# First batch's attention of a fused attention and mixture-of-experts kernel: where the exponentials are divided by their sums

## The chip, the cores and the metric

The kernel runs on one core of a Trainium2 chip. Its time is device microseconds of one launch, and the median of the runs of a kernel is what is compared. The engines are TensorE (PE in the profile, with its weight loads as PEld), VectorE (DVE), ScalarE (ACT), GpSimd (POOL) and SyncE (SP), which issues the DMAs.

## The reference, cut to what matters

Two batches, 8 heads, 768 positions, head dimension 64. Queries and keys that belong to the same of 16 clusters see each other; the result of the attention goes through two dense stages. Only the attention is touched by the change:

```python
    scores = scale * np.matmul(q, k.transpose(0, 1, 3, 2))
    scores = np.where(mask, scores, -1000000000.0)
    scores = scores - np.max(scores, axis=-1, keepdims=True)
    attn = np.exp(scores)
    attn = attn / (np.sum(attn, axis=-1, keepdims=True) + 1e-09)
    return np.matmul(attn, v).astype(np.float32)
...
    attn_out = _attn_ref(**attn_kwargs)
    x = np.ascontiguousarray(attn_out.transpose(0, 2, 1, 3)).reshape(B * S, H * D)
    x = _moe_ref(x=x, **moe_kwargs)
    return _moe2_ref(x=x, **moe2_kwargs)
```

## The kernel before, in words

The program is a list of tasks, each with an engine, a length, a priority and the buffers that it reads and writes. A planner in the kernel (`Order.plan`) places them one after the other by priorities and lengths from the table `PAR`, and the engines then run their instructions in that order, each engine strictly in its own. So a change of tasks or of numbers in the table moves instructions of all engines.

Batch 0 runs its attention alone at the start (up to about 150 us), beside the conversion of the dense weights (wconv), which fills gaps on ScalarE, GpSimd and VectorE. Then come the dense stages of batch 0, between whose products the attention of batch 1 is put, and the dense stages of batch 1.

The attention of batch 0 is the method `turned`. It works on pairs of heads (hp, four of them) and blocks of 256 queries (blk, three of them): 12 blocks, in the order of the list `seq`. A block has four units: two heads (q) by two groups of 128 queries (j). For a unit:

- TensorE makes the scores (pss, L827 and L829, 128 x 768 in two PSUM banks; two such buffers).
- VectorE takes the negated maximum of each row (L834), ScalarE the exponential with the sum of each row (e, L835; the trace shows the read of the sum as an instruction of its own).
- VectorE adds 1e-9 to the sum and takes the reciprocal (method `sums`, L843 and L844), and GpSimd multiplies the 128 x 768 exponentials with it in place (L735).
- TensorE turns them in six transposes (pst, L747, in two halves of three), and ScalarE (L754) or VectorE (L756) copies each half to SBUF (pt), by the letters of `kt`: A is ScalarE, D is VectorE.

When the four units of a block are there, TensorE multiplies values and turned exponentials (psv, L763): 12 products of 64 rows and 256 columns, the two heads into the two halves of the rows. They are issued in six parts. ScalarE takes the scaled high half of the result (x1h, L771) and VectorE the low half (x1l, L772), both from PSUM. The dense layer reads x1h and x1l (psg, L976 to L978).

New pairs of heads are prepared between the units: products with the centroids (psc, psct, pso), the splits of queries and keys (qa, ka, kb), and DMAs for them.

Of the kernel before, what the change touches and what calls it, by code (L numbers as in the profile page):

```python
# [9 lines left out]
F32 = mybir.dt.float32  # L10
# [11 lines left out]
PSC = 1024.0  # L22
# [5 lines left out]
def _f32(u):  # L28
# [14 lines left out]
    wx=-1.1522284557866715,  # L43
    wxs=1.4523186816394191,
    wx0=43.37150067903462,
    wl=7.46084025153843,
    slack=0.05,
    vre=2,
    nbv=12.297071615165793,
    nbr=16.02553508875921,  # L50
# [6 lines left out]
    ta=33.594464710837215,  # L57
    tu=2.610847985583524,
    lead0=24.37119650954177,
    lead2=1.612592269486031,  # L60
    vlead2=-5.510083383690325,
    lead1=2.0943943567986207,
    vlead=-47.653832407507394,
    avp=-10.148156292544726,
    parts=3,
    avpa=-4.563255851914643,
    kn='PPPPPP',
    kt='AAADA',
    kb='AAPD',
    gl=["DDDD", "DDDD"],  # L70
    mx=28.217289639625243,
    sp=15.01076876764054,
    spc=8.604011088911196,
    wse=dict(i="P", o="S", **{"1": "P", "2": "A"}),
    v0=9.16094046643471,
# [3 lines left out]
    v1=-23.758591458339424,  # L79
    a_pool=dict(raw=2, vr=4, sc=1, so=1, cs=2, oh=3, sm=2, e=7, pt=5, tiny=11, stk=4),  # L80
    b_pool=dict(raw=2, vr=2, sc=1, so=1, cs=1, oh=1, sm=2, e=2, p=3, pt=3, vh=1, vl=1, tiny=11, stk=2),
    xbb=1,
    loa="VP",
    lob="VV",
    r64p=2.853890633309904,
    slow=1.1738599594625483,
# [3 lines left out]
    trp=5.099669873070424,  # L90
    trh=2,
    parta=6,
    cv0=131.63876951108648,
    cvd=17.514404477757832,
# [10 lines left out]
    seq=[0, 1, 3, 2, 5, 4, 6, 7, 9, 10, 11, 8],  # L105
    btail=7.85293067823645,
    bu0=40.446540415353034,
    bdu=31.34254887856145,
    bvl=4.7901688951714965,
    bpr=6.264441884379736,  # L110
# [270 lines left out]
def body(ctx: ExitStack, tc: tile.TileContext, qk, vd, cent, w_in, w_out, probs, w1, w2, out):  # L381
# [33 lines left out]
    def pool(n, prio, fn, r, w, ns=2.1):  # L415
        return add("POOL", 1e-3 * (n * ns + 150), prio, fn, r, w, lk=True)
# [150 lines left out]
    class Attn:  # L567
# [824 lines left out]
```

## Time and profile before

| what | us |
|---|---|
| median of 3 runs | 969.84 |
| lowest and highest run | 967.96, 970.83 |
| profiled execution, its own time | 969.13 |
| its span, first to last instruction | 967.4 |
| TensorE busy (weight loads) | 923.6 (545.8) |
| VectorE, ScalarE, GpSimd busy | 737.5, 646.5, 361.6 |

The profiled execution is 1.7 us longer than its span and 0.7 us below the median. A busy TensorE is not one at its peak: a product counts from its start to its modelled end, so consecutive ones overlap in the trace, and what a product costs is read from start to start.

### The profile page before, as it was taken

The page shows a single profiled execution, that of the slowest core. Times are in us where ns is not written, and L with a number is a line of the kernel's source. Part 1 is how long each engine was busy: PE and PEld are TensorE (multiplying, and loading weights), DVE is VectorE, ACT ScalarE, POOL GpSimd, SP SyncE. Part 2 cuts the span into 40 slices and gives each one's busy share as a digit, 9 for nine tenths or more (in the row PEclk, how much of TensorE's full clock was granted, in tenths as well). Part 3 has the DMA queues.
Part 4 walks back from the last instruction along what each step waited for, and adds up shares of the span by engine and source line. Part 5 has one row for each costly group of instructions (what it writes and reads, how often), then busy time and mean ns, then how long its engine had stood idle before and what let it go on. Part 6 is the DMA issues. An engine that isn't in the chain of part 4 may idle for free.

```text
span 967.4 us, 16161 instructions
## 1 busy us (share of the span) xinstructions
PE 923.6 (95%) x5627; PEld 545.8 (56%) x5627; DVE 737.5 (76%) x1551; ACT 646.5 (67%) x1311; POOL 361.6 (37%) x394
## 2 busy tenths in 40 slices
PE   3999999999989998999999999999999999999998
PEld 1767765655545654555565565566654555555554
DVE  8988795887779898798898988945589666554543
ACT  5899986867776787787897755565466554555421
POOL 2566744324434346445354321101234442334100
PEclk9999999999999999999999999999999999999999
DMA  8343439785535465467466579332111212212001
GB/s 246 107 135 91 140 101 319 263 279 183 175 119 173 83 133 134 129 127 173 122 116 159 156 163 226 106 110 86 36 66 66 88 63 69 87 45 87 1 1 66
DMA packets 124369, 121.63 MB, mean 126 GB/s; under 512 B 81472, under 2 KB 81472, under 8 KB 124288
## 3 DMA queue, kind: packets, MB, share of 16 engines
q1 hardware_dynamic: 124288, 120.61, 43.8%
q8 instruction: 44, 0.72, 0.3%
q14 instruction: 37, 0.30, 0.1%
HBM read 81.32 MB, written 14.68 MB: 99 GB/s over the span
## 4 chain that ended last, share of the span: by engine, by line
PE 46%; DVE 6%; ACT 3%; DMA 1%; issue 1%; POOL 1%; SPq 0%; POOLq 0%; ACTq 0%
PE psm L976 6%; PE psm L977 6%; PE psm L978 6%; PE psw L1053 6%; PE psw L1055 6%; PE psw L1054 6%; PE psg L977 2%; PE psg L978 2%; PE psg L976 2%; PE pss L827 1%; DMA wraw<-in_w 1%; PE psv L809 1%; PE pss L829 1%; DVE h L1217 1%; ACT e L835 1%
## 5 line engine op out<-in xcount | busy, mean ns | idle before, releaser
L882 POOL TENSOR_TENSOR w<-wraw,w 128x512 f16<-128x512 f32 (+1 forms) x128 | 136.1, 1083 | 188.9 <-ACT w L881 146.9
L976 PE MATMUL psm<-w,h 128*128 128x512 f16 x384 | 146.1, 381 | 2.7 <-DVE h L1217 2.5
L978 PE MATMUL psm<-w,h 128*128 128x512 f16 x384 | 146.1, 380 | 0.5 <-DVE h L1217 0.5
L977 PE MATMUL psm<-w,h 128*128 128x512 f16 x384 | 145.9, 380 | 0.0
L835 ACT ACTIVATE e<-pss,ut 128x768 f32<-128x768 f32 x96 | 86.3, 900 | 26.8 <-DVE ut L834 24.7
L834 DVE TENSOR_REDUCE ut<-pss 128x1 f32<-128x768 f32 x96 | 91.3, 952 | 11.2 <-PE pss L829 9.8
L1063 ACT ACTIVATE keep<-psw 128x384 f32<-128x384 f32 x96 | 46.6, 486 | 60.1 <-PE psw L1055 59.5
L881 ACT ACTIVATE w<-wraw 128x512 f16<-128x512 f32 (+1 forms) x128 | 71.7, 580 | 21.2 <-POOL wraw L880 12.4
L880 POOL TENSOR_SCALAR wraw<-wraw,wsc 128x512 f32<-128x512 f32 x64 | 48.3, 762 | 98.3 <-DVE ws L938 30.8
L976 PE MATMUL psg<-g,w 128*128 128x384 f16 x256 | 83.5, 326 | 1.4 <-DVE t L1124 1.2
L977 PE MATMUL psg<-g,w 128*128 128x384 f16 x256 | 83.4, 326 | 1.4 <-DVE g L1126 1.4
L978 PE MATMUL psg<-g,w 128*128 128x384 f16 x256 | 83.5, 326 | 0.0
L1239 DVE SCALAR_TENSOR_TENSOR oa<-psm,pq,oa 128x512 f32<-128x512 f32 x84 | 61.9, 744 | 23.6 <-PE psm L978 23.5
L977 PEld LDWEIGHTS <-w 128*128 128x128 f16 x512 | 50.1, 98 | 36.6 <-issue 5.4
L978 PEld LDWEIGHTS <-w 128*128 128x128 f16 x512 | 50.1, 98 | 36.0 <-issue 3.0
L976 PEld LDWEIGHTS <-w 128*128 128x128 f16 x512 | 50.7, 99 | 33.4 <-issue 1.7
L827 PE MATMUL pss<-ka,qa 128*128 128x384 f32 x192 | 61.5, 402 | 3.7 <-ACT e L835 3.1
L1217 DVE SCALAR_TENSOR_TENSOR h<-psw,h 128x384 f16<-128x384 f32 x78 | 42.9, 552 | 27.8 <-ACT h L1216 27.6
L978 PEld LDWEIGHTS <-h 128*128 128x128 f16 x384 | 37.6, 98 | 46.3 <-DVE h L1217 1.0
L1054 PE MATMUL psw<-tx,ws 128*128 128x384 f16 x192 | 63.0, 328 | 0.8 <-DVE tx L1005 0.8
L1053 PE MATMUL psw<-tx,ws 128*128 128x384 f16 x192 | 63.1, 328 | 0.7 <-ACT tx L1004 0.6
L1055 PE MATMUL psw<-tx,ws 128*128 128x384 f16 x192 | 63.0, 328 | 0.0
(198 smaller groups left out, 2370.1 us busy)
## 6 DMA issues: line engine op xcount, KB each, us to landing
wraw<-in_w SPq DMA_DIRECT2D x128, 256.0 KB, 3.5
r<-in_w_in SPq DMA_DIRECT2D x16, 512.0 KB, 4.5
r<-in_w_out SPq DMA_DIRECT2D x16, 512.0 KB, 4.6
w<-hl_i SPq DMA_DIRECT2D x32, 256.0 KB, 3.0
w<-hl_o SPq DMA_DIRECT2D x32, 256.0 KB, 4.0
raw<-in_qk SPq DMA_DIRECT2D x16, 384.0 KB, 3.9
vr<-in_vd SPq DMA_DIRECT2D x12, 384.0 KB, 4.1
hl_i<-w SPq DMA_DIRECT2D x16, 256.0 KB, 2.4
```

Source lines behind the costliest of these rows:

```text
L827: nc.tensor.matmul(ps[:, f, 0:HS], qa[:, qs], ka[:, f * HS:f * HS + HS], start=True, stop=False)
L834: dve(S, p, lambda: nc.vector.tensor_reduce(out=nb(), in_=ps[:, :, 0:HS], axis=AX.XY, op=ALU.max, negate=True), [ps], [(tb, n)])
L835: act(S, p, lambda: nc.scalar.activation(out=e.t.rearrange("p (a b) -> p a b", a=2), in_=ps[:, :, 0:HS], func=AF.Exp, bias=nb(), scale=1.0 ...
L881: act(c, p, lambda w=w, raw=raw, c=c: nc.scalar.activation(out=w[:, 0, 0:c], in_=raw[:, 0:c], func=AF.Copy), [raw], [(w, 0)])
L882: pool(c, p, lambda w=w, raw=raw, c=c: nc.gpsimd.tensor_tensor(out=w[:, 1, 0:c], in0=raw[:, 0:c], in1=w[:, 0, 0:c], op=ALU.subtract), [raw ...
L976: nc.tensor.matmul(o_, ah, bh, start=i == 0, stop=False)
L977: nc.tensor.matmul(o_, ah, bl, start=False, stop=False)
L978: nc.tensor.matmul(o_, al, bh, start=False, stop=i == 3)
L1053: nc.tensor.matmul(o_, ah, bh, start=not more and k == 0, stop=False, skip_group_check=more)
L1054: nc.tensor.matmul(o_, ah, bl, start=False, stop=False, skip_group_check=more)
L1055: nc.tensor.matmul(o_, al, bh, start=False, stop=k == 1, skip_group_check=more)
L1239: dve(512, p, lambda: nc.vector.scalar_tensor_tensor(out=oa[:, t], in0=ps.t, scalar=q, in1=oa[:, t], op0=ALU.mult, op1=ALU.add), [ps, qk], ...
```

## The change

In `turned` the exponentials of a unit are no longer multiplied with the reciprocals of their sums; the transposes read them as the exponential left them. The sums of the four units of a block lie in one tile (ut), and `sums` runs once on its four columns. Four new products (L763 in the new numbering, function `over`) multiply each column of reciprocals, repeated 64 times, with the 128 x 128 identity: the result has the reciprocal of query k in column k of each of 64 rows. They go to columns 256 to 511 of the PSUM tile psv, whose columns 0 to 255 take the product with values. ScalarE copies them to SBUF (r, with the scale that the result had), VectorE multiplies the product with values by r (u), ScalarE takes the high half from u, and GpSimd subtracts it for the low half. The letters of `kt` give VectorE 3 copies in 10 instead of 1 in 5, the order of blocks `seq` differs in two places, and most real numbers of the planner's table differ.

```diff
-    kn='PPPPPP',
-    kt='AAADA',
+    xl0='P',
+    kt='AADAAAADAD',
...
-    seq=[0, 1, 3, 2, 5, 4, 6, 7, 9, 10, 11, 8],
+    seq=[0, 1, 3, 5, 2, 4, 6, 7, 9, 10, 8, 11],
...
+            tb = self.buf("tiny", [128, 8], F32, "ut")
...
-                    tb = self.buf("tiny", [128, 8], F32, "ut")
-                    e = self.scores(qa, qb, ka, kb, blk * BQ + j * 128, tb, 0, p(i))
-                    self.sums(tb, 1, p(i), 1.0)
-                    sc = lambda eng, e=e, tb=tb: eng.tensor_scalar(out=e.t, in0=e.t, scalar1=tb[:, 2:3], scalar2=1.0, op0=ALU.mult, op1=ALU.mult)
-                    if PAR["kn"][i % len(PAR["kn"])] == "P":
-                        pool(S, p(i), lambda sc=sc: sc(nc.gpsimd), [(tb, 2)], [e], ns=0.956)
-                    else:
-                        dve(S, p(i), lambda sc=sc: sc(nc.vector), [(tb, 2)], [e], fast=True)
+                    e = self.scores(qa, qb, ka, kb, blk * BQ + j * 128, tb, i, p(i), 4)
...
-            ps = Buf(p_v[b], [128, BQ], F32, "psv")
+            ps = Buf(p_v[b], [128, 2 * BQ], F32, "psv")
...
+            def over():
+                for j in range(JQ):
+                    for q in range(2):
+                        c = BQ + 128 * j
+                        nc.tensor.matmul(ps[64 * q:64 * q + 64, c:c + 128], tb[:, 4 + q * JQ + j:5 + q * JQ + j].to_broadcast([128, 64]), ident.t,
+                                         start=True, stop=True, skip_group_check=True)
...
+            self.sums(tb, 2 * JQ, p(4), 1.0, 4)
+            pe(JQ * 0.235, p(4) + avp, over, [(tb, 4 + i) for i in range(2 * JQ)], [(ps, 1)], JQ * 512)
...
-            act(BQ, p(6), lambda: nc.scalar.activation(out=xh[:, hp, sl], in_=ps.t, func=AF.Copy, scale=sc), [ps, ks], [(xh, key)], ps=True, ap=True)
-            dve(BQ, p(6), lambda: nc.vector.scalar_tensor_tensor(
-                out=xl[:, hp, sl], in0=ps.t, scalar=sc, in1=xh[:, hp, sl], op0=ALU.mult, op1=ALU.subtract), [ps, ks, (xh, key)], [(xl, key)], ap=True)
+            u, r = self.buf("u", [128, BQ], F32), self.buf("u", [128, BQ], F32, "r")
+            act(BQ, p(5), lambda: nc.scalar.activation(out=r.t, in_=ps[:, BQ:2 * BQ], func=AF.Copy, scale=sc), [(ps, 1), ks], [r], ps=True, ap=True)
+            dve(BQ, p(6), lambda: nc.vector.tensor_tensor(out=u.t, in0=ps[:, 0:BQ], in1=r.t, op=ALU.mult), [(ps, 0), r], [u])
+            act(BQ, p(6), lambda: nc.scalar.activation(out=xh[:, hp, sl], in_=u.t, func=AF.Copy), [u], [(xh, key)])
+            low = lambda eng: eng.tensor_tensor(out=xl[:, hp, sl], in0=u.t, in1=xh[:, hp, sl], op=ALU.subtract)
+            if PAR["xl0"] == "P":
+                pool(BQ, p(6), lambda: low(nc.gpsimd), [u, (xh, key)], [(xl, key)])
```

In the planned order, TensorE's rows around the third block's product with values, before (pst the transposes, pss the scores, psv the product with values; an x behind a row counts instructions):

```order
L747 MATMUL pst<-ident,e 128x128 x6
L827 MATMUL pss<-ka,qa 128x384 x2
L829 MATMUL pss<-kb,qb 128x384 x2
L747 MATMUL pst<-ident,e 128x128 x3
L763 MATMUL psv<-pt,vr 64x256 x12
L747 MATMUL pst<-ident,e 128x128 x6
```

The same place after, in the new line numbers, where psv<-ident,ut are the four products that spread the reciprocals:

```order
L741 MATMUL pst<-ident,e 128x128 x3
L836 MATMUL pss<-ka,qa 128x384 x2
L838 MATMUL pss<-kb,qb 128x384 x2
L741 MATMUL pst<-ident,e 128x128 x6
L763 MATMUL psv<-ident,ut 64x128 x4
L836 MATMUL pss<-ka,qa 128x384 x2
L838 MATMUL pss<-kb,qb 128x384 x2
L757 MATMUL psv<-pt,vr 64x256 x12
L741 MATMUL pst<-ident,e 128x128 x6
```

The four products came in behind the last transposes of the block, apart from the product with values; of the 12 sets one, the last, stands directly ahead of its product with values.

VectorE's rows at the same time, before (L834 the maximum, L843 the addition, L844 the reciprocal, L959 to L963 the conversion of weights, L772 the low half):

```order
L843 TENSOR_SCALAR ut<-ut 128x1
L844 RECIPROCAL ut<-ut 128x1
L772 SCALAR_TENSOR_TENSOR x1l_585<-psv,vm,x1h_571 128x256
L834 TENSOR_REDUCE ut<-pss 128x1
L756 COPY pt<-pst 128x384
L834 TENSOR_REDUCE ut<-pss 128x1
L843 TENSOR_SCALAR ut<-ut 128x1
```

and after, for the third block (L843 is now the maximum, L852 the addition and L853 the reciprocal on four columns, L968 and L970 the conversion, L750 the copy):

```order
L843 TENSOR_REDUCE ut<-pss 128x1
L968 TENSOR_SCALAR wconv<-wconv 128x512
L970 SCALAR_TENSOR_TENSOR wconv<-r_615,wconv 128x512
L852 TENSOR_SCALAR ut<-ut 128x4
L843 TENSOR_REDUCE ut<-pss 128x1
L853 RECIPROCAL ut<-ut 128x4
L843 TENSOR_REDUCE ut<-pss 128x1
L750 COPY pt<-pst 128x384
```

Addition and reciprocal stand once per block now, and here a maximum stands between the two.

## Rows read from the trace of the kernel before

**Rows 1.** Stretches: us, busy of PE, PEld, DVE, ACT, POOL; PEclk, DMA, GB/s
```profile
29.60:149.20 119.60, 113.22 (x824) 84.55 (x823) 103.23 (x245) 110.21 (x246) 69.62 (x76) 1.00 0.39 117
150.00:200.00 50.00, 50.00 (x313) 30.46 (x312) 33.83 (x71) 36.75 (x72) 22.43 (x28) 1.00 0.86 301
200.00:300.00 100.00, 94.54 (x567) 55.19 (x566) 81.51 (x164) 74.97 (x156) 39.95 (x48) 0.98 0.55 183
```

**Rows 2.** Timeline of PE from 82 us: start, us, instruction; scores and transposes
```profile
82.92 0.60 PE L827 MATMUL pss<-ka,qa 128*128 128x384 f32 x2
...
83.70 0.82 PE L747 MATMUL pst<-ident,e 128*128 128x128 f32 x6
84.35 0.44 PE L827 MATMUL pss<-ka,qa 128*128 128x384 f32 x1
```

**Rows 3.** Timeline of PE from 95.6 us: the product with values and its neighbours
```profile
96.51 0.49 PE L747 MATMUL pst<-ident,e 128*128 128x128 f32 x3
96.93 2.81 PE L763 MATMUL psv<-pt,vr 128*64 128x256 f32 x24
99.68 0.88 PE L747 MATMUL pst<-ident,e 128*128 128x128 f32 x6
```

**Rows 4.** Timeline of PE, three short stretches inside that product
```profile
97.20 0.60 PE L763 MATMUL psv<-pt,vr 128*64 128x256 f32 x4
...
97.42 0.60 PE L763 MATMUL psv<-pt,vr 128*64 128x256 f32 x4
...
99.36 0.39 PE L763 MATMUL psv<-pt,vr 128*64 128x256 f32 x2
```

**Rows 5.** Groups by line, PE, 29.6 to 147.1 us: busy, mean ns, idle before
```profile
L747 PE MATMUL pst<-ident,e 128*128 128x128 f32 x279 | 40.9, 278 | 3.0 <-POOL e L735 1.9 <-POOL wconv L957 0.6 <-ACT pt L754 0.5
L763 PE MATMUL psv<-pt,vr 128*64 128x256 f32 x288 | 34.0, 383 | 0.0
L827 PE MATMUL pss<-ka,qa 128*128 128x384 f32 x88 | 26.6, 384 | 2.0 <-ACT e L835 1.5
...
L977 PE MATMUL psg<-x1l,w 128*128 128x384 f16 x11 | 3.6, 326 | 0.0
...
L632 PE MATMUL psc<-raw,ct 128*32 128x384 f32 x16 | 1.7, 498 | 0.0
L683 PE MATMUL pso<-ident_b,oh 128*64 128x128 bf16 x18 | 1.5, 222 | 0.0
```

**Rows 6.** Waits, 29.6 to 149.5 us: who for whom, total us, times, longest
```profile
PEld pss L827 <- ACT e L835: 5.5, 15, 1.0
...
PEld pst L747 <- POOL e L735: 3.6, 7, 1.5
...
PE pst L747 <- POOL e L735: 1.9, 3, 1.1
...
PEld pst L747 <- POOL wconv L957: 0.8, 1, 0.8
```

**Rows 7.** Groups by line, 25 to 150 us, of POOL and ACT
```profile
L735 POOL TENSOR_SCALAR e<-e,ut 128x768 f32<-128x768 f32 x48 | 45.9, 960 | 36.3 <-DVE ut L843 11.1 <-DVE wconv L959 3.7 <-PE pss L829 3.4
...
L754 ACT ACTIVATE pt<-pst 128x384 f32<-128x384 f32 x76 | 34.8, 493 | 3.3 <-PE pst L747 3.1
...
L771 ACT ACTIVATE x1h<-psv,vm 128x256 f16<-128x256 f32 x12 | 5.7, 473 | 1.1 <-PE psv L763 1.0
```

**Rows 8.** Timeline of all engines from 96.6 us: a maximum, and exponential to reciprocal
```profile
96.71 0.96 DVE L834 TENSOR_REDUCE ut<-pss 128x1 f32<-128x768 f32 x1 [0.19 <-PE pss L829]
...
97.76 0.90 ACT L835 ACTIVATE e<-pss,ut 128x768 f32<-128x768 f32 x1 [0.48 <-DVE ut L834]
...
98.79 0.15 DVE L843 TENSOR_SCALAR ut<-ut 128x1 f32<-128x1 f32 x1 [0.39 <-ACT e L835]
98.97 0.17 DVE L844 RECIPROCAL ut<-ut 128x1 f32<-128x1 f32 x1
```

**Rows 9.** Line L961, 25 to 150 us: durations in ns, min, median, max
```profile
L961 DVE SCALAR_TENSOR_TENSOR wconv<-r,wconv x16: 668/683/1086, 31.8 to 149.1; 128x512 int32<-128x512 int32 x16
```

More of the change, by code (lines that the diff above doesn't have):

```diff
@@ L56 @@
     wgap=4,
[L57 to L64, printed above, removed]
+    ta=37.644627171937636,
+    tu=2.618105922827514,
+    lead0=23.811664523217768,
+    lead2=1.3177589412550317,
+    vlead2=-6.734196292615577,
+    lead1=1.6382475212753322,
+    vlead=-81.01415307879348,
+    avp=-14.807207563391803,
     parts=3,
-    avpa=-4.563255851914643,
-    kn='PPPPPP',
-    kt='AAADA',
+    avpa=-5.248976072211778,
+    xl0='P',
+    kt='AADAAAADAD',
     kb='AAPD',
     gl=["DDDD", "DDDD"],
-    mx=28.217289639625243,
-    sp=15.01076876764054,
-    spc=8.604011088911196,
+    mx=28.184025027324456,
+    sp=14.78416087479403,
+    spc=2.4836840744754025,
     wse=dict(i="P", o="S", **{"1": "P", "2": "A"}),
-    v0=9.16094046643471,
+    v0=17.35296956647561,
     lr=0.3,
@@ L89 @@
     dpx=2,
[L90 removed]
+    trp=4.004466787339696,
     trh=2,
     parta=6,
[L93 to L94 removed]
+    cv0=132.11254764398825,
+    cvd=17.98889306697888,
     cva=2,
@@ L762, in av @@
                     for q in range(2):
-                        nc.tensor.matmul(ps[64 * q:64 * q + 64], vr[:, q, t], pts[q][:, :, t], start=t == 0, stop=t == NT - 1)
+                        nc.tensor.matmul(ps[64 * q:64 * q + 64, 0:BQ], vr[:, q, t], pts[q][:, :, t], start=t == 0, stop=t == NT - 1, skip_group_check=True)
+            def over():
[4 more added lines that the diff above has]
+                                         start=True, stop=True, skip_group_check=True)
             for part in range(parts):
-                pe(NT / parts * (BQ * 4 / 2400 + 0.02), p(4 + part * 4 / parts) + avp, lambda part=part: av(part), pts + [vr], [ps], NT / parts * BQ * 4)
+                pe(NT / parts * (BQ * 4 / 2400 + 0.02), p(4 + part * 4 / parts) + avp, lambda part=part: av(part), pts + [vr], [(ps, 0)], NT / parts * BQ * 4)
+            self.sums(tb, 2 * JQ, p(4), 1.0, 4)
+            pe(JQ * 0.235, p(4) + avp, over, [(tb, 4 + i) for i in range(2 * JQ)], [(ps, 1)], JQ * 512)
             sl = slice(blk * BQ, blk * BQ + BQ)
@@ L819, in block, with scores @@
                 out=xl[:, hp, sl], in0=ps.t, scalar=col, in1=xh[:, hp, sl], op0=ALU.mult, op1=ALU.subtract), [ps, (xh, key)], [(xl, key)])
-        def scores(self, qa, qb, ka, kb, q0, tb, n, p):
+        def scores(self, qa, qb, ka, kb, q0, tb, n, p, s0=2):
             ps = Buf(p_s[self.b], [128, 2, 512], F32, "pss")
@@ L836, in scores, with sums @@
                 out=e.t.rearrange("p (a b) -> p a b", a=2), in_=ps[:, :, 0:HS], func=AF.Exp, bias=nb(), scale=1.0, accum_out=rs()),
-                [ps, (tb, n)], [e, (tb, 2 + n)], ps=True, acc=True, tab=AF.Exp)
+                [ps, (tb, n)], [e, (tb, s0 + n)], ps=True, acc=True, tab=AF.Exp)
             return e
-        def sums(self, tb, n, p, unit=1.0 / PSC):
-            keys = [(tb, 2 + i) for i in range(n)]
-            rs = lambda: tb[:, 2:2 + n]
+        def sums(self, tb, n, p, unit=1.0 / PSC, s0=2):
+            keys = [(tb, s0 + i) for i in range(n)]
+            rs = lambda: tb[:, s0:s0 + n]
             dve(n, p, lambda: nc.vector.tensor_scalar(out=rs(), in0=rs(), scalar1=1e-9, scalar2=unit, op0=ALU.add, op1=ALU.mult), [], keys)
```

32 lines of the change are left out of this document (17 added, 15 removed).

## The prediction

> **What bounds the kernel now.** I read the stages first: busy time of each engine by stretch [rows 1]. From 29.6 us, when the scores run one after the other, to 149.2 us, when the first dense layer takes over, TensorE is busy 113.2 of 119.6 us, ScalarE 110.2, VectorE 103.2 and GpSimd 69.6. Behind it, from 150 to 200 us, TensorE is busy 50.0 of 50.0. So the stage that the change touches has a full TensorE directly behind it, and what the stage gains or loses in time on TensorE goes into the span.
>
> Busy time alone says little, since a product counts as busy until its modelled end. So I read from starts what TensorE needs at least. One set of scores starts at 82.92 and the transposes behind it at 83.70: 0.78 us. Six transposes take until 84.35: 0.65 us, 0.108 each [rows 2]. The product with values, 24 entries of 256 columns, starts at 96.93 and the next transposes at 99.68: 2.75 us. Three transposes ahead of it take 0.42 (96.51 to 96.93) where three elsewhere take 0.33: 0.09 more [rows 3]. Then I count [rows 5]: 279 transposes at 0.108 are 30.1; 88 entries of the first scores line are 44 sets, at 0.78 34.3; 288 entries of psv are 12 products, at 2.84 34.1; 33 of the dense layer's psg at 50.00 / 313 = 0.16 [rows 1] are 5.3 (the row of one of its three lines has 11); psc 1.7, pso at most 18 x 0.108 = 1.9. With psct and psn (under 1) that is 108 of the 119.5 us from 29.64 to 149.19. TensorE stands only some 11 us in the whole stage. **It is the bound here**, with ScalarE close behind, and a change that gives it work must find that work in these 11 us.
>
> Who takes the 11 us stands in the waits [rows 6]: the scores wait 5.5 us at the weight load for an exponential that frees their PSUM buffer; the transposes wait 3.6 us at the load, of which 1.9 stay visible at the product, for the scaling on GpSimd (0.8 more are put down to a conversion that shares GpSimd with it).
>
> **The change part by part.**
>
> *Out: the scaling.* 48 multiplications of 0.960 us on GpSimd go [rows 7], 45.9 us of an engine that is not the bound. They stood between exponential and transposes, so with them go the transposes' waits. At least the visible 1.9 us return, at most 3.6 + 0.8 = 4.4 [rows 6]. I take 4.0, near the upper end, since the load's wait is what the product behind it inherits. Next late there is the exponential itself.
>
> *Out: three of four normalisations.* The two small VectorE steps run once per block on four columns instead of four times on one: 36 reciprocals of about 0.17 us and as many additions of about 0.15 [rows 8], together some 11 us. Eight of 96 copies of the turned exponentials move from ScalarE (0.493 each) to VectorE, and the multiply u takes the place of the low half x1l there. VectorE ends some 6 us lighter of 103. It is not the bound; what it can give is an earlier maximum, so an earlier exponential, so less of the 5.5 us. Between 0 and 5.5, I take 1.0.
>
> *ScalarE.* New: the copy r of the spread reciprocals, 12 of about 0.473 (the nearest row is x1h, which reads as many columns from PSUM [rows 7]), 5.7 us. Gone: eight copies, 3.9 us. x1h now reads SBUF, between nothing and 0.2 us less each. ScalarE stays where it was, 110 of 120: so most of the wait for exponentials stays, which is why I take only 1.0 above. The 12 low halves x1l go to GpSimd, which has room for them, and nothing on TensorE reads them within the stage apart from the first dense products.
>
> *In: the spread.* Per block four products of 128 columns into halves of 64 rows, eight entries as the trace counts (psv has 24 entries for 12 products). Before shows no such product; the nearest is the product with values. Its entries go in pairs: four that start at 97.20 are followed by four that start at 97.42, a step of 0.22 for two entries of 256 columns [rows 4]. Half the columns: 0.11, and four steps are 0.44 us. Entering costs the 0.09 above, and 0.05 since the first step is 0.27 (96.93 to 97.20). Leaving costs 0.10: the last pair starts at 99.36 and the transposes at 99.68, 0.32 instead of 0.22. Sum 0.68. Lower bound 0.44, if entering and leaving are hidden; upper bound 0.88 + 0.24 = 1.12, if an entry costs the same whatever its columns. I take 0.68, by the row that it is most like. In the order only the last of the 12 stands directly ahead of its product with values; 11 are alone between full-width products. So 12 x 0.44 + 11 x 0.24 = **7.9 us**, from 5.3 to 13.4. TensorE gets no work less, so this term cannot fall below nothing.
>
> The trace shows cost in proportion to columns: 0.108 for 128 full-width columns and 0.22 for a pair of 256 [rows 2, 4]. The Trainium skill, TensorEngine Tiling (Array Packing), Performance Considerations, Instruction Overhead, gives each matmul about 60 cycles on top. By it, as an estimate from that page, four steps of 25 ns make 0.1 us per block, 1.2 us in all, and the sum would end 1.2 us higher; the rows show no such part.
>
> *In: a wait.* TensorE works in order, and the spread waits for the reciprocal. From the end of an exponential it takes the read of the sum, the addition and the reciprocal: 98.66 to 99.14, 0.48 us [rows 8]. The order above shows a maximum (0.96 us, [rows 8]) between addition and reciprocal in the third block: 1.4 us, of which the six transposes of the same exponential hide 0.65. Some 0.8 us would be left there, and queued behind it on TensorE are the next scores and the product with values. In most blocks one or two sets of scores and transposes more (1.43 each) stand ahead and cover it. Between 0 and 12 x 0.8 = 9.6; I take 0.15 per block, 1.8, as the cover is there in most.
>
> **Sum:** 7.9 + 1.8 - 4.0 - 1.0 = +4.7 us. The profiled execution took 969.13 (span 967.4 and 1.7 around it), 0.7 under the median of 969.84; 969.13 + 4.7 = 973.8 beside a profiled run, and 974.5 beside the median. The moved numbers of the planner's table change little behind the stage: the order of TensorE from the dense layer on is the same but for some places in the second batch's attention. I cost that at nothing, with 2 us either way in the range.
>
> **The rivals.**
>
> *Faster: the chain tightens.* If TensorE's waits shrink to below 11 - 7.9, about 3 us, the stage ends earlier. The mechanism: with no scaling between, exponentials and transposes run ahead, and a lighter VectorE and GpSimd give maxima sooner, so the 5.5 us go as well. With 10 of the 11 us recovered and the spread at its lower bound, 5.3 - 10 = -4.7: 965.1. For it: both waits belong to the same loop. Against it: ScalarE stays as full as before, and it is ScalarE that frees the scores' buffer.
>
> Of two VectorE steps that read two SBUF tensors, L961 took 0.668 us at least and 1.086 at most, with a median of 0.683 [rows 9]: few of its 16 were held up, and GpSimd's silence is worth little to VectorE, at most 8 x 0.42 = 3.3 us on this line (half of them lie at or below the median). The Trainium skill, SBUF — State Buffer, SBUF: two separate sides, says that such a step and a GpSimd instruction exclude each other for a whole instruction; by that rule this rival gains those 3.3 us at most, on VectorE, which is not the bound.
>
> *No change: the delay is taken up behind.* From 200 to 300 us TensorE idles 100 - 94.5 = 5.5 us [rows 1]. If those waits hung on something that doesn't move with the stage, a transfer for instance, 4.7 us of delay would vanish in them: 970. Against it: they end on VectorE steps of the same dense chain, which moves along.
>
> *Much slower: the reciprocals decide.* If the 0.8 us stood in every block, 9.6 instead of 1.8: +12.5, 982.3. For it: VectorE works in order and the order puts maxima and conversions around the two small steps. That the change doesn't do what it says is out: the order shows 12 spreads.
>
> **How the numbers follow.** Forecast 0.47 (its own range 971.5 to 979: the spread between 0.5 and 0.9 a block, the returned waits between 1.9 and 5.4). Much slower 0.10, no change 0.22, faster 0.21. A measurement of this kernel tells about 0.3%, 2.9 us, from no change: below 966.9 is faster, above 972.7 slower. Some of the forecast's lower end and all of the no-change case lie within: faster 0.21, same 0.25, slower 0.54. The range leaves out half of the faster case's tail and the top of the slower one: 965 to 981.
>
> **What would show it.** Right: eight entries per block at about 0.11 a pair step, a spread that costs 0.6 to 0.7 us from its start to the next full-width product less what it waits; no wait of transposes for GpSimd; waits of scores for exponentials still of 3 us and more; the dense layer's unbroken run begins some 5 us later than at 149.2. Wrong: TensorE's waits in the stage below 3 us, a spread of under 0.45 us, or a dense run that begins later while the span does not grow.

## The result, and the profile after

The changed kernel took 982.94 us in the median of 4 runs (982.23 to 985.01), the kernel before 970.17 beside it: a ratio of 1.0139, 95% interval 1.0116 to 1.0163. Predicted were 974.5, from 965 to 981. The direction was right, the loss was 12.8 us instead of 4.7. The profiled execution took 983.61 us, its span 981.8. It lies 14.5 us above the profiled execution of before (969.13), the medians 12.8 apart: of the four runs of the changed kernel the profiled one is one of two with a mean granted clock of 0.992 (983.61 and 985.01), the others took 982.27 and 982.23 at 0.997 and 0.998.

The stage after, as the first of [rows 1] (us; busy of PE, PEld, DVE, ACT, POOL; PEclk, DMA share, GB/s), up to where the dense layer takes over:

```profile
29.60:163.70 134.10, 121.86 (x917) 90.88 (x918) 105.11 (x185) 113.56 (x252) 34.43 (x43) 0.99 0.37 114
```

The stage is 14.5 us longer (134.1 for 119.6), TensorE in it only 8.6 us busier. The dense layer's unbroken run shows in both timelines of PE by the same stop ahead of it; the first row is before, the second after:

```profile
149.19 0.32 PE L976 MATMUL psg<-x1h,w 128*128 128x384 f16 x1 [1.35 <-DVE t L1124]
```

```profile
163.69 0.32 PE L985 MATMUL psg<-x1h,w 128*128 128x384 f16 x1 [1.35 <-DVE t L1133]
```

14.5 us later, and the span grew by 14.4: in these two traces nothing was taken up behind. So the whole question lies in the stage. The third block's spread in PE's timeline of after (start, duration), where [rows 3] showed the product with values alone:

```profile
48.64 0.60 PE L741 MATMUL pst<-ident,e 128*128 128x128 f32 x3
49.17 0.66 PE L763 MATMUL psv<-ident,ut 128*64 128x128 f32 x8
49.76 0.88 PE L741 MATMUL pst<-ident,e 128*128 128x128 f32 x6
50.39 0.59 PE L836 MATMUL pss<-ka,qa 128*128 128x384 f32 x2
50.81 0.51 PE L838 MATMUL pss<-kb,qb 80*128 80x384 f32 x2
51.26 2.81 PE L757 MATMUL psv<-pt,vr 128*64 128x256 f32 x24
```

Eight entries, 0.59 us from their start to the transposes: as forecast. What the forecast did not have stands in the waits from 29.6 to 164 us (who for whom: us in all, times, longest), which answer to [rows 6]:

```profile
PEld pss L836 <- ACT e L844: 7.7, 12, 1.6
...
PEld psv L757 <- ACT r L775: 5.0, 8, 1.1
PE pss L836 <- ACT e L844: 4.7, 9, 1.3
...
PEld pst L741 <- DVE pt L750: 3.0, 3, 2.0
PE psv L757 <- ACT r L775: 2.5, 4, 0.8
...
PEld psv L763 <- DVE ut L853: 2.3, 3, 1.1
...
PE pst L741 <- DVE pt L750: 1.7, 1, 1.7
...
PE psv L763 <- DVE ut L853: 1.3, 2, 0.8
```

The transposes' wait for GpSimd is gone. In its place the scores wait longer for exponentials (7.7 at the load, 4.7 left at the product, for 5.5 [rows 6] and 1.5 [rows 5]), the product with values waits for ScalarE's copy r, though it writes other columns of the tile psv than r reads, and transposes wait for VectorE's copies.

Both waits of the spread for reciprocals that are left at TensorE, 0.52 and 0.82 us, have a cause that the forecast did not name. Of the 12 additions on four columns ten take 0.16 or 0.17 us, and the two ahead of these waits 1.19 and 1.55: each ends as an instruction of GpSimd (kb, for a new pair of heads) ends. The first of them, in the timelines of POOL, DVE and PE:

```profile
78.90 1.81 POOL L617 TENSOR_TENSOR kb<-raw,ka 64x768 fp32r<-64x768 f32 x1 [1.75 <-DMA qb<-so]
```

```profile
79.55 1.19 DVE L852 TENSOR_SCALAR ut<-ut 128x4 f32<-128x4 f32 x1
```

```profile
81.01 0.66 PE L763 MATMUL psv<-ident,ut 128*64 128x128 f32 x8 [0.52 <-DVE ut L853]
```

Nearly half of the loss is there early. Two windows, before and then after:

```profile
14.00:45.00 31.00, 26.00 (x148) 19.30 (x147) 27.73 (x63) 23.53 (x49) 14.79 (x15) 1.00 0.56 154
```

```profile
14.00:45.00 31.00, 22.07 (x126) 16.19 (x124) 26.30 (x47) 22.71 (x46) 8.66 (x10) 1.00 0.58 164
```

TensorE has 126 entries behind it by 45 us where it had 148, the first spread's 8 among them. The second product with values starts at 51.26, as shown above, and before it starts at 44.68, 6.6 us earlier:

```profile
44.68 2.81 PE L763 MATMUL psv<-pt,vr 128*64 128x256 f32 x24
```

The largest single stop of TensorE behind 29.6 us is this, PE and then VectorE in the timelines of after:

```profile
42.02 0.52 PE L838 MATMUL pss<-kb,qb 80*128 80x384 f32 x2
44.19 0.88 PE L741 MATMUL pst<-ident,e 128*128 128x128 f32 x6 [1.66 <-DVE pt L750]
...
45.71 1.48 PE L741 MATMUL pst<-ident,e 128*128 128x128 f32 x6
47.19 1.01 PE L836 MATMUL pss<-ka,qa 128*128 128x384 f32 x2
```

```profile
37.11 0.96 DVE L843 TENSOR_REDUCE ut<-pss 128x1 f32<-128x768 f32 x1
40.34 1.19 DVE L968 TENSOR_SCALAR wconv<-wconv 128x512 int32<-128x512 int32 x2 [2.28 <-POOL wconv L966]
41.45 1.28 DVE L970 SCALAR_TENSOR_TENSOR wconv<-r,wconv 128x512 int32<-128x512 int32 x2
42.65 0.68 DVE L972 SCALAR_TENSOR_TENSOR wconv<-r,wconv 128x512 int32<-128x512 int32 x1
43.26 0.41 DVE L776 TENSOR_TENSOR u<-psv,r 128x256 f32<-128x256 f32 x1
43.59 0.54 DVE L750 COPY pt<-pst 128x384 f32<-128x384 f32 x1
```

VectorE stands 2.28 us for a conversion step of GpSimd, then does five conversion steps and u, and the copy on which TensorE's transposes wait comes behind all of them. The reader is to see the price of an engine's strict order: the copy itself takes 0.54.

### The profile page after: what moved, and what is told of

Read it like the earlier page. It is cut to its first block, busy times and chain, and to the rows that moved or that the text cites. A ratio compares the mean times of both kernels' runs of the same rounds, so it can differ in the third digit from the quotient of the medians.

```text
span 981.8 us, 16175 instructions
## 1 busy us (share of the span) xinstructions
PE 934.2 (95%) x5723; PEld 552.5 (56%) x5723; DVE 738.7 (75%) x1487; ACT 648.8 (66%) x1315; POOL 326.7 (33%) x358
## 4 chain that ended last, share of the span: by engine, by line
PE 66%; DVE 17%; ACT 7%; DMA 4%; issue 3%; POOL 2%; SPq 0%; POOLq 0%; ACTq 0%; DVEq 0%
PE psm L985 7%; PE psm L986 7%; PE psm L987 7%; PE psw L1062 6%; PE psw L1063 6%; PE psw L1064 6%; PE psg L985 5%; PE psg L986 5%; PE psg L987 5%; PE psv L757 3%; PE pss L836 3%; DMA wraw<-in_w 2%; PE pst L741 2%; PE pss L838 2%; DVE ut L843 2%
## 5 line engine op out<-in xcount | busy, mean ns | idle before, releaser
L844 ACT ACTIVATE e<-pss,ut 128x768 f32<-128x768 f32 x96 | 86.2, 898 | 28.1 <-DVE ut L843 25.9
L843 DVE TENSOR_REDUCE ut<-pss 128x1 f32<-128x768 f32 x96 | 91.2, 952 | 13.0 <-PE pss L838 11.2
```

What stands on the lines that cost most here:

```text
L843: dve(S, p, lambda: nc.vector.tensor_reduce(out=nb(), in_=ps[:, :, 0:HS], axis=AX.XY, op=ALU.max, negate=True), [ps], [(tb, n)])
L844: act(S, p, lambda: nc.scalar.activation(out=e.t.rearrange("p (a b) -> p a b", a=2), in_=ps[:, :, 0:HS], func=AF.Exp, bias=nb(), scale=1.0 ...
```

## The experiments

Medians are beside a before of 969.4 to 970.8 in the same sets; ratios are to before, with 95% intervals. Theory A: the division's own work and waits on TensorE are the loss. Theory B: it is the new order. Both came to be refined.

**Division left out, planned anew.** The sums, the spread, r and u go, the halves are taken from psv as before; the rest is the changed kernel.

```diff
-            self.sums(tb, 2 * JQ, p(4), 1.0, 4)
-            pe(JQ * 0.235, p(4) + avp, over, [(tb, 4 + i) for i in range(2 * JQ)], [(ps, 1)], JQ * 512)
...
-            act(BQ, p(5), lambda: nc.scalar.activation(out=r.t, in_=ps[:, BQ:2 * BQ], func=AF.Copy, scale=sc), [(ps, 1), ks], [r], ps=True, ap=True)
-            dve(BQ, p(6), lambda: nc.vector.tensor_tensor(out=u.t, in0=ps[:, 0:BQ], in1=r.t, op=ALU.mult), [(ps, 0), r], [u])
```

> The changed kernel without the division: no sums, no spread products, no r and u; the high and low halves are taken from the product with values as before (so the result is not divided by the sums). Theory: TensorE bounds the stage, and of the 14.5 us by which the dense layer resumes later in the changed kernel's trace, the spread takes 12 x 0.68 = 8 us, its waits for the reciprocals 1.5 and the product with values' waits for r 2.9. All go: 982.9 - 12.4 = about 970.5, or 968 if the lighter ScalarE also shortens the waits for exponentials. Rival: the planner's new numbers and the order that follows make the loss, whatever the spread does: above 976.

Measured 979.71, ratio 1.0097 (1.0073 to 1.0121). Some 9 of the 12.8 us are there without any division. But the planner had arranged all tasks anew, so an edit of the tasks tests two things at once. Behind the next three, most kernels keep an order: the tasks stay, and only what they issue is changed.

**Spread twice, apart, and by DMA (all planned anew).** The four products issued twice; the spread in a buffer of the transposes (pst) and not in the product's tile; the spread by DMAs through memory instead of TensorE, without the copy r.

The edits, one after the other:

```diff
+            pe(JQ * 0.235, p(4) + avp, over, [(tb, 4 + i) for i in range(2 * JQ)], [(ps, 1)], JQ * 512)
```

```diff
+            pr_ = Buf(p_tr, [128, 2 * BQ], F32, "psr")
...
-                        nc.tensor.matmul(ps[64 * q:64 * q + 64, c:c + 128], tb[:, 4 + q * JQ + j:5 + q * JQ + j].to_broadcast([128, 64]), ident.t,
+                        nc.tensor.matmul(pr_[64 * q:64 * q + 64, c:c + 128], tb[:, 4 + q * JQ + j:5 + q * JQ + j].to_broadcast([128, 64]), ident.t,
```

```diff
-            pe(JQ * 0.235, p(4) + avp, over, [(tb, 4 + i) for i in range(2 * JQ)], [(ps, 1)], JQ * 512)
+            dma(40e3, p(4), lambda: nc.sync.dma_start(out=scr.t.rearrange("c k -> k c"), in_=tb[:, 4:4 + 2 * JQ]), [(tb, 4 + i) for i in range(2 * JQ)], [scr])
+            for q in range(2):
+                dma(66e3, p(4), lambda q=q: nc.sync.dma_start(
+                    out=r[64 * q:64 * q + 64], in_=scr.t[q * JQ:q * JQ + JQ].rearrange("j k -> (j k)").unsqueeze(0).to_broadcast([64, BQ])), [scr], [(r, q)])
```

> The changed kernel with the four spread products issued twice in a row (the second set writes the same values again). Theory: TensorE bounds the stage, so four more pair steps of 0.11 us in each of 12 blocks go into the time whole: +5.3 us, 988.2; up to +8 (991) if a set also pays entering and leaving again. Rival: TensorE has room here and the loss lies in waits of other engines: +1 us or less, 984.

> The changed kernel with the spread in a PSUM buffer of the transposes and no longer in the bank of the product with values. Theory: the product with values waits for ScalarE's copy r only because both lie in one tile (2.9 us visible on TensorE in the trace); the wait goes, 980, unless the transposes, which have one buffer less for that time, give it back. Rival: the wait stands for a full ScalarE, and the same time comes back as a wait of scores for exponentials: 982 to 984.

> The changed kernel with the reciprocals spread by DMAs (a 128 x 4 tile is written to DRAM turned, and read back repeated to 64 rows for each head) instead of the products with the identity; no copy r on ScalarE, u takes the scale itself. Theory: TensorE loses the 8 us of the spread and the waits of 1.5 and 2.9 us, ScalarE 12 copies of 0.47: about 970, and 966 to 968 if waits for exponentials shrink too. Rival: the transfers, some 2 us each and one behind the other in a queue that also brings weights, hold u, so the only buffer of the product with values comes free late and the next block's product waits: 975 or more.

Measured 995.51 (1.0238 to 1.0298), 987.0 (1.0147 to 1.0185) and 1066.85 (1.0976 to 1.101). A second spread costs some 12 us, about 1 a block, more than the 0.68 of the sum; the plan is another one again, so this is not the price of the products alone. Apart, the product's wait for r is gone, but the transposes lose a buffer, and it is 4 us worse; what of this is the buffer and what the plan is not separated. By DMA, VectorE and with it ScalarE stand for the transfer, in the waits of that kernel from 29.6 to 210 us:

```profile
DVE u L774 <- DMA r<-rcp: 54.2, 8, 11.4
...
ACT x1h L775 <- DVE u L774: 34.2, 6, 10.7
```

**Four parts alone, each in an unchanged order.** The spread added to the kernel before (with columns of the identity for reciprocals); the changed kernel without the spread; the changed kernel with r read from SBUF; the kernel before with one column scaled on GpSimd.

The edits, one after the other (the second kernel has the third's edit too; cuts inside an edit are marked by dots):

```diff
+                if part == 0:
+                    for j in range(JQ):
+                        for q in range(2):
+                            c = BQ + 128 * j
+                            nc.tensor.matmul(ps[64 * q:64 * q + 64, c:c + 128], ident[:, j:j + 1].to_broadcast([128, 64]), ident.t,
+                                             start=True, stop=True, skip_group_check=True)
```

```diff
             def over():
+                return
```

```diff
-            act(BQ, p(5), lambda: nc.scalar.activation(out=r.t, in_=ps[:, BQ:2 * BQ], func=AF.Copy, scale=sc), [(ps, 1), ks], [r], ps=True, ap=True)
+            act(BQ, p(5), lambda: nc.scalar.activation(out=r.t, in_=vr[:, 0, 0:4].rearrange("p t d -> p (t d)"), func=AF.Copy, scale=sc), [(ps, 1), ks], [r], ps=True, ap=True)
```

```diff
+                    sc1 = lambda eng, e=e, tb=tb: eng.tensor_scalar(out=e[:, 0:1], in0=e[:, 0:1], scalar1=tb[:, 2:3], scalar2=1.0, op0=ALU.mult, op1=ALU.mult)
...
-                        pool(S, p(i), lambda sc=sc: sc(nc.gpsimd), [(tb, 2)], [e], ns=0.956)
+                        pool(S, p(i), lambda sc=sc1: sc(nc.gpsimd), [(tb, 2)], [e], ns=0.956)
```

> The kernel before, its order and its scaling kept, with one thing added: ahead of each product with values the four products with the identity are issued into columns 256 to 511 of the same PSUM tile, with columns of the identity in the place of reciprocals, so that they wait for nothing, and nothing reads them. The 12 sets cost TensorE 12 x 0.68 = 8.2 us by the trace of the changed kernel. Theory A (TensorE has no room, the spread's work passes whole into the time): 970.3 + 8 = 977 to 979. Rival C (part of the 11 idle us of the stage takes it up): 970 to 974.

> The changed kernel with every engine's order kept as it is, but the four products of each block are not issued, and ScalarE's copy r reads the values from SBUF instead of the spread reciprocals; so the division is left out. What goes: the products (8.2 us), TensorE's waits for the reciprocals (1.5) and for the copy r (2.9). Theory A (these three are the loss): 982.9 - 12.6 = 969 to 972. Theory B (the order that the new numbers of the table give is slower by itself, as the first look at a planned-anew kernel without division, 979.7, suggests): 975 or more.

> The changed kernel with every engine's order kept and the spread issued, but ScalarE's copy r reads the values from SBUF and not the spread reciprocals from the tile of the product; the division is left out. Only the wait of the product with values for that copy goes: 2.9 us seen at TensorE. If that wait costs what the trace shows: 979 to 980.5. If another wait (the copies of the turned exponentials that end at the same time) stands right behind it: 982 to 983.

> The kernel before with its order kept, but GpSimd scales one of the 768 columns of each unit's exponentials, so that the wait of the transposes for the sums stays and GpSimd's 0.96 us is cut short; the division is left out in the other columns. This is what the change takes away, alone. My prediction put it at 4.0 us (1.9 to 4.4): 965 to 968.5. Rival (the next wait takes its place at once): 969.5 to 970.5.

| kernel | us | ratio, interval |
|---|---|---|
| before, spread added | 977.19 | 1.0058 (1.0039 to 1.0077) |
| after, no spread, r from SBUF | 977.22 | 1.0058 (1.0042 to 1.0074) |
| after, r from SBUF | 981.48 | 1.0102 (1.0081 to 1.0122) |
| before, one column scaled | 967.86 | 0.9978 (0.9961 to 0.9995) |

The spread's work costs 6 us where it has no waits of its own, and the scaling gives 2 to 3 (0.5 to 3.8 by the interval; some waits of transposes for GpSimd are left in that kernel, 0.4 us at the product). The wait for r costs 1.5 by the medians and some 3.5 by the ratios, and this interval meets that of the changed kernel. Without the spread and without TensorE's waits for the reciprocals and for r, the changed kernel still stands at 977: 6 of its 12.8 us remain, although the scaling is out of it as well, which alone gives 2 to 3. The same window shows a delay without any division; in this trace a first input transfer came late and set TensorE back by 1.5 us against the changed kernel's, and the rest comes with the order:

```profile
14.00:45.00 31.00, 20.77 (x110) 14.37 (x108) 24.76 (x44) 21.55 (x43) 7.58 (x9) 1.00 0.59 173
```

The second and third kernel differ by the spread and its waits for reciprocals alone: 981.48 less 977.22, 4.3 us, some 2 to 7 by the intervals, so no more than in the order of before and perhaps less. In part the spread fills waits that are there without it, as the scores' waits for exponentials at the product show, without the spread and then with it:

```profile
PE pss L836 <- ACT e L844: 7.6, 14, 1.4
```

```profile
PE pss L836 <- ACT e L844: 5.0, 10, 0.8
```

**Numbers against code.** The old code with the new table, the new code with the old table, block order and copy letters, both planned anew.

Of the edit of the second (the first puts the same values in the other way), some lines of some thirty:

```diff
-    nbv=1.942240026658137,
+    nbv=12.297071615165793,
...
-    kt='AADAAAADAD',
+    kt='AAADA',
...
-    seq=[0, 1, 3, 5, 2, 4, 6, 7, 9, 10, 8, 11],
+    seq=[0, 1, 3, 2, 5, 4, 6, 7, 9, 10, 11, 8],
```

> The code before (scaling on GpSimd, no spread) with the numbers, block order and copy letters of the changed kernel's table, planned anew. Theory B1 (the new numbers make the slower order): 976 or more. Theory B2 (the new code makes it: with GpSimd's scaling gone the planner finds VectorE and GpSimd free early and puts conversions of weights there, 19 conversion steps on VectorE ahead of the third block's last maximum and 22 ahead of the fourth's, where before has 9 and 12; this kernel has 9 and 13): 969 to 973.

> The changed code with the numbers, block order and copy letters of the table before, planned anew. Its conversions stand as far ahead as in the changed kernel (16 steps on VectorE ahead of the third block's last maximum, 22 ahead of the fourth's). Theory B1 (new numbers make the loss): 976 to 978, before plus the spread's work and its waits. Theory B2 (the code and the early conversions make it): 981 or more.

Measured 987.93 (1.0159 to 1.0203) and 983.16 (1.0116 to 1.0157). Both readings fall in part: the new code takes the same time with either table, so the loss does not need the new numbers, block order and copy letters; but the old code loses 18 us by the table alone, with the conversions about as far ahead as before has them. What an order can cost in this kernel is more than any term of the division.

**Conversions spaced out.** Loads of the weights 8 us apart, and the same with r on VectorE.

```diff
-                out=r.t, in_=src[:, k].bitcast(I32).rearrange("p (n t) -> p n t", t=2)), [], [r], start=G["nbr"])
+                out=r.t, in_=src[:, k].bitcast(I32).rearrange("p (n t) -> p n t", t=2)), [], [r], start=22 + 8.0 * (4 * wi + k))
```

```diff
-            act(BQ, p(5), lambda: nc.scalar.activation(out=r.t, in_=ps[:, BQ:2 * BQ], func=AF.Copy, scale=sc), [(ps, 1), ks], [r], ps=True, ap=True)
+            dve(BQ, p(5), lambda: nc.vector.tensor_scalar(out=r.t, in0=ps[:, BQ:2 * BQ], scalar1=sc, scalar2=None, op0=ALU.mult), [(ps, 1), ks], [r], ap=True)
```

> The changed kernel, with one edit for the planner: the loads of the weights to be converted may start no earlier than 22 us and then 8 us apart, so that the conversion steps stand as far ahead as in the kernel before (on VectorE 9 ahead of the third block's last maximum and 12 ahead of the fourth's, where the changed kernel has 19 and 22). Everything of the division stays. Theory B2 (early conversions ahead of maxima and copies cost about 7 us, as TensorE's progress by 52 us suggests): 975 to 978. Theory A (the division's own work and waits are the loss): 981 to 984.

> As the kernel with spaced conversions, and the copy r of the spread reciprocals is made by VectorE instead of ScalarE (12 of about 0.45 us). If ScalarE's 5.7 us of copies hold up the exponentials: 2 to 4 us below the kernel with spaced conversions. If VectorE, which then has the copy between maxima, is as late: within 1 us of it.

Measured 1022.07 (1.0515 to 1.0557) and 1023.73 (1.0537 to 1.0599). Neither tells its theories apart: the late weights starve the dense layers, as the waits of PE from 200 to 320 us in the first of them show.

```profile
PE psg L985 <- DMA w<-hl_o: 13.3, 2, 11.1
PE psg L985 <- DMA w<-hl_i: 11.3, 2, 10.4
```

**Short conversions.** In both kernels, in their orders, the three VectorE steps of the first eight conversions on 16 of 512 columns. The edit of the first of the three steps:

```diff
-                out=a(), in0=a(), scalar1=3, scalar2=0x3FFFFFFF, op0=ALU.logical_shift_left, op1=ALU.bitwise_and), [], [raw], fast=True)
+                out=a()[:, 0:few], in0=a()[:, 0:few], scalar1=3, scalar2=0x3FFFFFFF, op0=ALU.logical_shift_left, op1=ALU.bitwise_and), [], [raw], fast=True)
```

> The changed kernel in its order, with the three VectorE steps of each of the first eight weight conversions done on 16 of 512 columns, so 24 steps of 0.42 to 0.69 us become short; the rest of these weights is left unconverted. If the conversion steps that stand ahead of maxima and copies make the loss of 7 us by 52 us: 974 to 977, six or more below the changed kernel, while the same edit in the kernel before gains 2 at most. If not: both fall alike.

> The kernel before in its order, with the same edit: the three VectorE steps of the first eight weight conversions on 16 of 512 columns. There they stand spread over the first 100 us. If conversions ahead of maxima are what the changed kernel suffers from: 968 to 970 here, since they were hidden. If VectorE's load as such sets the end in both: as far below as in the changed kernel with this edit.

Measured 979.76 (1.0062 to 1.0145) for after and 969.26 (0.997 to 1.0007) for before. After gains some 3 us, before 0.8. In the trace of the first the transposes' wait for VectorE's copy at 44 us is gone, and the second product with values starts at 48.28, where the changed kernel's starts at 51.26. It points to the conversions ahead of VectorE's copies and maxima, for two or three us of the loss and not for all; the interval meets that of the changed kernel, so this is not shown.

**The whole division in the old order.** The tasks and order of before; the scaling issues nothing, the spread follows the product with values, and r, u, the high half and the low half stand where the halves stood.

```diff
+                if part == parts - 1:
+                    for j in range(JQ):
+                        for q in range(2):
+                            c = BQ + 128 * j
+                            nc.tensor.matmul(ps[64 * q:64 * q + 64, c:c + 128], tbs[q * JQ + j][:, 2:3].to_broadcast([128, 64]), ident.t,
+                                             start=True, stop=True, skip_group_check=True)
...
+            def high():
+                nc.scalar.activation(out=u[:, BQ:2 * BQ], in_=ps[:, BQ:2 * BQ], func=AF.Copy, scale=sc)
+                nc.vector.tensor_tensor(out=u[:, 0:BQ], in0=ps[:, 0:BQ], in1=u[:, BQ:2 * BQ], op=ALU.mult)
+                nc.scalar.activation(out=xh[:, hp, sl], in_=u[:, 0:BQ], func=AF.Copy)
```

> The whole new division in the planned order of the kernel before: no scaling on GpSimd, the four products that spread the reciprocals right behind the last part of each product with values, the copy r on ScalarE, the multiply u on VectorE, the high half from u, the low half on GpSimd; table, block order, copy letters, the reciprocals of one unit each and all other rows stand as in the kernel before. Theory O (the division's own terms are about as my sum had them, and the rest of the loss is the order in which the planner put the changed tasks): before + 6.4 (spread, measured alone) - 2.9 (scaling, measured alone) + 0 to 2 (waits for r): 973 to 976. Theory A (the division's own waits make the loss in any order): 980 or more.

Measured 981.61 (1.0077 to 1.0146). Theory O fell as stated: the old order alone does not save it. Theory A is met by its number, but the next kernels show that the place of the steps still decides. The waits from 29.6 to 164 us point to it (u in ACT's rows is the copy of the reciprocals, L781):

```profile
DVE u L782 <- ACT u L781: 13.8, 12, 2.2
...
PEld pst L748 <- ACT pt L755: 8.9, 12, 1.3
...
ACT x1h L783 <- DVE u L782: 5.9, 12, 0.5
PE pst L748 <- ACT pt L755: 5.2, 11, 0.9
...
ACT u L781 <- PE psv L769: 4.4, 8, 1.5
```

In 8 of 12 blocks ScalarE stands for the spread, in all 12 for VectorE's multiply, and the copies of the turned exponentials queue behind it. One block in ACT's timeline:

```profile
104.37 0.47 ACT L781 ACTIVATE u<-psv,vm 128x256 f32<-128x256 f32 x1 [0.44 <-PE psv L769]
105.34 0.42 ACT L783 ACTIVATE x1h<-u 128x256 f16<-128x256 f32 x1 [0.49 <-DVE u L782]
105.66 0.85 ACT L755 ACTIVATE pt<-pst 128x384 f32<-128x384 f32 x2
```

**The same, with the steps moved by one place.** The spread ahead of the product; multiply, high half and low half one ScalarE instruction later. And that kernel without the copy r. The edit is against the kernel just above:

```diff
-                if part == parts - 1:
+                if part == 0:
...
+            def low():
                 nc.vector.tensor_tensor(out=u[:, 0:BQ], in0=ps[:, 0:BQ], in1=u[:, BQ:2 * BQ], op=ALU.mult)
                 nc.scalar.activation(out=xh[:, hp, sl], in_=u[:, 0:BQ], func=AF.Copy)
+                nc.gpsimd.tensor_tensor(out=xl[:, hp, sl], in0=u[:, 0:BQ], in1=xh[:, hp, sl], op=ALU.subtract)
```

And in the second:

```diff
             def high():
-                nc.scalar.activation(out=u[:, BQ:2 * BQ], in_=ps[:, BQ:2 * BQ], func=AF.Copy, scale=sc)
+                return
...
-                nc.vector.tensor_tensor(out=u[:, 0:BQ], in0=ps[:, 0:BQ], in1=u[:, BQ:2 * BQ], op=ALU.mult)
+                nc.vector.tensor_tensor(out=u[:, 0:BQ], in0=ps[:, 0:BQ], in1=vr[:, 0, 0:4].rearrange("p t d -> p (t d)"), op=ALU.mult)
```

> The whole new division in the order of the kernel before, as in the first such kernel, but so that ScalarE and VectorE need not stand at it: the four products that spread the reciprocals ahead of the product with values, only the copy r in the place of the old high half on ScalarE, and multiply, new high half and low half in the place of the old low half, one ScalarE instruction later. There ScalarE had waited 5.9 us for the multiply and 4.4 for the spread, VectorE 13.8 for r, and transposes 7.2 us for the copies behind. Theory W (the loss in the old order is these waits of two nearly full engines): spread 6.4 - scaling 2.9 + some 1 to 3 for the copy r: 974 to 977. Theory L (ScalarE's and TensorE's added work makes it, wherever it stands): 980 or more.

> The same kernel without the copy r on ScalarE (12 of 0.47 us): the multiply takes the values from SBUF in its place, so the division is left out, and the spread is issued but not used. What this falls below the kernel with the copy is the price of 5.7 us more on ScalarE: 1 to 4 us if ScalarE, which frees the scores' buffer, has no room; under 1 us if it has.

Measured 976.3 (1.0041 to 1.0087) and 975.03 (1.0036 to 1.0081). The first does all that the changed kernel does and is 6.6 us faster than it; the intervals don't touch. Its waits, as above:

```profile
PEld pss L843 <- ACT e L851: 7.6, 19, 1.0
...
PEld pst L748 <- ACT pt L755: 5.1, 11, 1.0
...
PE pss L843 <- ACT e L851: 2.9, 6, 0.7
...
PE pst L748 <- ACT pt L755: 2.3, 5, 0.7
```

ScalarE's 5.9 us for the multiply are gone from the list, and the transposes' visible wait has fallen from 5.2 to 2.3. Theory W holds, for the two moves together: the spread's place and the later steps were not tried apart. The spread in its timeline of PE:

```profile
150.13 0.66 PE L766 MATMUL psv<-ident,ut 128*64 128x128 f32 x8
150.62 2.76 PE L770 MATMUL psv<-pt,vr 128*64 128x256 f32 x24
```

The medians differ by 1.3 us for the copy r, but the intervals overlap almost whole, so a price of r as ScalarE's work is not shown.

The bill: from before to the moved steps +6.0 (all of the division, well placed), from there to the changed kernel +6.6 (place and order of the steps, with the copy letters and the sums of four units at once that belong to that order and were not tried apart). The first could not be made a gain here: the scaling gives back less than the spread takes, in the order of before as well. No version that does the whole division beat the kernel before.

## Why the prediction was right or wrong, point by point

- **TensorE is the bound, and what the stage loses goes into the span:** right. 14.5 us there, 14.4 in the span. The rival by which the delay is taken up behind is out, and so is the faster one, since TensorE's waits in the stage grew.
- **Spread, 7.9 us (5.3 to 13.4):** right in the rows (0.59 from the start of the eight entries to the transposes, as 0.44, 0.05 and 0.10 had it), too high in the time. In the kernel before with the spread added, all 12 stand directly ahead of their products, where they take 0.49 each, 5.9 in all, and 6 was measured, with part of it in waits that were there: the transposes' wait for GpSimd at the load falls from 3.6 to 2.4. In the changed kernel's own order the spread and its reciprocals together are worth 4.3 us, some 2 to 7 by the intervals, where the sum had 7.9 and 1.8. "TensorE gets no work less" is right, but the scores' waits for exponentials were there to take some of the work up. The higher price by the Trainium skill (TensorEngine Tiling (Array Packing), Performance Considerations, Instruction Overhead: about 60 cycles of overhead for each matmul) shows in no row: in the kernel with moved steps the spread takes 0.49 up to the product, which is the four steps of 0.11 and the 0.05 of the first.
- **Scaling out, −4.0 (1.9 to 4.4):** the right wait, taken too high: 2 to 3 us alone, within the stated bounds.
- **Waits for reciprocals, +1.8:** right in size, 1.3 left at the product and 2.3 at the load, but by another mechanism, so by luck: the 1.3 us are not a maximum between addition and reciprocal but two additions that ended only as GpSimd's kb did. And the rival whose 982.3 comes nearest was right by its number only: it wanted 9.6 us there.
- **A lighter VectorE, −1.0:** wrong in sign. VectorE's steps were lighter by some 4 us, and by the 6 of the sum but for the two long additions shown above. The scores' wait for exponentials left at the product went from 1.5 to 4.7 in the changed kernel, and to 2.9 even in the well placed one.
- **GpSimd's silence:** right to count it for little, though what GpSimd still does held up two additions and so TensorE, as shown above. The two-tensor step of the conversion took 0.668 to 1.086 us with a median of 0.683 [rows 9]; after, its 16 took 0.679 to 0.695 with a median of 0.684. Only the longest went, and no gain of it shows at TensorE. By the Trainium skill (SBUF — State Buffer, SBUF: two separate sides), such a step and a GpSimd instruction that reads SBUF keep each other out for a whole instruction; that the longest steps go with GpSimd's scaling agrees with it.
- **ScalarE stays where it was, and r has a price of nothing beyond its busy time:** wrong. r brought a wait of the product with values (2.5 us left at the product; in the time 1.5 to 3.5, not clear of noise), which the sum did not have, since I asked for what r waits and not for who waits for r.
- **The step that failed:** "The moved numbers of the planner's table change little behind the stage ... I cost that at nothing, with 2 us either way". I looked for moved rows behind the stage and costed none inside it. There the planner arranged the stage anew, conversions ahead of copies and maxima among it, and this was worth 6.6 us: the same division in the order of before, well placed, loses 6.0, near the 4.7 of the sum, and the changed kernel 12.8. The table's numbers, which I named, are not needed for it: with the old ones the new code takes the same time. Why that order loses is open in part: the conversions on VectorE may account for two or three us, but the intervals meet, so that is not shown.

## What to carry to other kernels

A step that is put on the critical engine costs its rows, but a step that is put between two nearly full engines costs what stands behind it in each: the same division took 981.6 or 976.3 us by whether the spread stood behind or ahead of the product and whether ScalarE and VectorE reached the steps behind it at once or one instruction later. For a kernel with a planned order, cost the order inside the changed stage too: a change of tasks rearranges it, and here that was as dear as the change itself. To tell the two apart, keep the old order and change only what its tasks issue.

## What the runs showed of the hardware

I had not expected the clock to fall in this stage. In the profiled run of the changed kernel, after TensorE had stood 1.66 us ahead of 44.19, its granted clock was near the lower of its two levels, 1.2 GHz, for a few microseconds:

```profile
45.20:48.90 3.70, 3.70 (x16) 3.11 (x15) 2.94 (x8) 3.31 (x9) 0.07 (x1) 0.54 0.74 245
```

Six transposes and the set of scores behind them took 1.48 and 1.45 us from start to start, where [rows 2] have 0.65 and 0.78: 1.5 us on top of the stop itself. The scores end with the transposes' start at 48.64, shown above. Before, the stage's granted clock is 1.00 [rows 1].

The stop alone does not bring the fall. In the changed kernel with r from SBUF, TensorE stands as long for the same copy. The second six transposes behind the stop take 0.82 us there, where the row at 45.71 above has 1.48, and the granted clock from 44 to 50 us is 1.00:

```profile
46.42 0.87 PE L741 MATMUL pst<-ident,e 128*128 128x128 f32 x6 [1.62 <-DVE pt L750]
...
47.84 0.82 PE L741 MATMUL pst<-ident,e 128*128 128x128 f32 x6
```

What else it takes stays open here.

And ScalarE's read of one half of a PSUM tile held up TensorE's products into the other half: the first product with values starts at 37.83, after 0.77 us of standing, as the copy r ends (37.33 and 0.46 long).

```profile
37.33 0.46 ACT L775 ACTIVATE r<-psv,vm 128x256 f32<-128x256 f32 x1
```

```profile
37.83 3.19 PE L757 MATMUL psv<-pt,vr 128*64 128x256 f32 x24 [0.77 <-ACT r L775]
```

With r read from SBUF this wait is gone from the list. Whether the chip or the program's semaphores keep the two apart was not tried.
